# Casting transfers for v and z, paired half key tiles, and the experts' rows turned on VectorE

## The chip, the cores and the metric

The kernel runs on one core of a Trainium2 chip. TensorE multiplies, VectorE and ScalarE work on elements, GpSimd and SyncE (SP) issue transfers; GpSimd's queue also carries the gathers and scatters of the experts' rows. The metric is the device time of one execution in microseconds (us). Before the change three executions took 2464.53, 2465.4 and 2467.0 us: a median of 2465.4.

## What is computed

Eight batches of 2496 rows go through an attention without softmax, and then all 19,968 rows through a mixture of eight experts, each of which takes exactly 2496 rows.

```python
scores = (1.0 / S) * np.matmul(z, z.transpose(0, 2, 1))     # z: 8 x 2496 x 64
attn   = np.maximum(scores, 0.0) ** 2
x      = (u * np.matmul(attn, v)).reshape(B * S, D)         # u, v: 8 x 2496 x 256
logits = x @ w_gate                                         # 256 x 8
# the (row, expert) pairs in falling order of logit; a row goes to the first
# expert that still has room (room for N // E = 2496 rows each)
for e in range(E):
    mask = assigned == e
    h = np.maximum(x[mask] @ w1[e], 0.0)                    # 256 x 1024
    out[mask] = h @ w2[e]                                   # 1024 x 256
```

Everything is fp32.

## The kernel before

**Precision.** An fp32 operand is split into a high part, rounded to float32r, and a low part, the difference. A product is three matmuls: high by high, high by low, low by high. In the names `vh`, `vl`, `hi`, `lo`, `xh`, `xl` the h and l stand for the parts.

**Attention.** A batch has 20 key tiles: 19 of 128 rows and a last one of 64 (`NT` = 19, `TL` = 64). Queries go in five groups, four of 512 columns and one of 448. For each of the 40 groups and 20 key tiles there is a step n. `scores` multiplies key tiles in pairs, since the contraction has only 64 rows: one tile on rows 0 to 63 of the array, one on rows 64 to 127 (L961), three matmuls each. `rectify` takes the scores from PSUM, on ScalarE (L973) or VectorE (L971); ScalarE squares (L977); `split_hi` and `split_lo` make `hi` (L982 on ScalarE, L984 on VectorE) and `lo` (L993). `av` multiplies with v into two accumulators `acc`, one for each half of v's 256 columns (L1006, L1008, L1009). Of the half key tile the scores stand twice, on rows 0 to 63 and on 64 to 127; `split_lo` turns rows 64 to 127 of `hi` into the low part in place (L990), and `av` takes vh by both at once and vl by hi: four matmuls over 128 rows.

All scores of a group are issued in one burst of 60 matmuls, `LA` = 4 steps ahead of its first `av`. `hi` and `lo` have `LA` + 1 = 5 buffers. v and z of the next batch are split while the last query group of a batch runs: `load_v` and `load_z` fetch on SP, `split_v` rounds `vh` on ScalarE (L943) and subtracts `vl` on VectorE (L944), `split_z` likewise (L935, L936). `vh` and `vl` have `RING` = 22 buffers for 20 tiles. In that group the `hi` of even tiles is made on VectorE. After a group, VectorE turns the result in 32x32 blocks (`turn_acc`, L1015), multiplies with u (L1021), and SP writes it to `xd` in DRAM and reads it back as rows `xs`, of which VectorE makes eight logits per tile (`post_logits`, L1045). In the attention the order on TensorE, ScalarE and VectorE is the order in which this code is written (`manual_schedule`); the lists `todo` and `first_in` say at which step the loads, splits and logits stand. The order on SP and GpSimd is a scheduler's.

**Experts.** Each expert has 5 groups of rows with 8 steps each: 320 steps in all. GpSimd gathers a group's rows from `xd` (`gather_x`, L590, 4 gathers of 128 rows), TensorE transposes them into PSUM (`turn_x`, L642, 8 transposes into `xp` and `hp`), ScalarE and VectorE split them (L646, L647). A step computes a tile of the hidden layer in `hp` (L652 to L654), splits it (L730, L732) and, three steps later, multiplies it into `y` (L745 to L750). `put_y` adds the parts of y on VectorE (L773) and GpSimd scatters the rows (L781). Beside that VectorE and TensorE work out which rows the next expert gets (`route`: L124, L286 to L289, L523, L529 and others). The number of that expert comes into `which`, and `load_w` fetches its weights on SP. `todo` gives the step of each gather, turning and split; the scheduler sets the order within, and some operations are tied behind the last `hl` (L732) by `issue_after(paced[-1].ins)`.

## Time and profile before

| | |
|---|---|
| median of three executions | 2465.4 us (2464.53 to 2467.0) |
| profiled execution | 2466.28 us, span 2464.5 us |
| mean granted TensorE clock | 0.996 |
| TensorE busy | 2416.7 us, 98% |
| VectorE busy | 2067.0 us, 84% |
| ScalarE busy | 1535.1 us, 62% |
| GpSimd busy | 362.5 us, 15% |

The page gives busy times over the whole span, the chain of work that ended last (each instruction is followed back to what released it), and the costliest groups of instructions. Busy is not the same as limiting: an engine may be 84% busy over the span, and full in one stretch and half idle in another. The trace answers by stretch: busy time of each engine in a window, the single instructions with their starts, and who waited for whom. A wait counts only if it lies on the engine that sets the end.

### The profile page before, as it was taken

How to read it: one execution, taken by the hardware profiler on the slowest of the kernel's cores; microseconds unless marked ns; L12 is line 12 of the kernel's file. 1: busy time of each engine (PE TensorE's matmuls, PEld its weight loads, DVE VectorE, ACT ScalarE, POOL GpSimd, SP SyncE). 2: the span in 40 equal slices, each digit the busy share in tenths (PEclk: the TensorE clock that was granted, in tenths of full speed). 3: DMA queues.
4: the chain of work that ended last, by engine and by line, in shares of the span. 5: the costliest groups of instructions: out<-in, count | busy, mean ns of one | idle time of the engine just before them, and what ended most of it. 6: DMA issues, size and time to landing. Idle time of an engine off the chain costs nothing.

```text
span 2464.5 us, 42329 instructions
## 1 busy us (share of the span) xinstructions
PE 2416.7 (98%) x14948; PEld 2016.6 (82%) x14948; DVE 2067.0 (84%) x6309; ACT 1535.1 (62%) x2986; POOL 362.5 (15%) x508
## 2 busy tenths in 40 slices
PE   8999999999999999999999899999999999999997
PEld 6888888888888888888887787788888888888886
DVE  7899898998999998989989897879796969696332
ACT  7898888898898988888987123333333333343332
POOL 3000000000000000000000022233242433333332
PEclk9999999999999999999999999999999999999999
DMA  4132131131131321312211022121212111122111
GB/s 150 34 105 62 52 114 30 53 110 52 45 109 37 100 66 52 114 27 55 76 52 43 9 70 69 34 73 47 70 51 69 44 64 54 45 86 68 43 42 34
DMA packets 156852, 154.86 MB, mean 63 GB/s; under 512 B 89440, under 2 KB 129888, under 8 KB 156512
## 3 DMA queue, kind: packets, MB, share of 16 engines
q1 hardware_dynamic: 141408, 110.72, 15.1%
q0 software_dynamic: 15232, 41.44, 5.3%
q8 instruction: 117, 1.92, 0.3%
q14 instruction: 95, 0.78, 0.1%
HBM read 111.22 MB, written 40.89 MB: 62 GB/s over the span
## 4 chain that ended last, share of the span: by engine, by line
PE 86%; DVE 8%; issue 3%; ACT 1%; DMA 1%; POOL 1%; POOLq 0%; ACTq 0%; DVEq 0%; SPq 0%
PE acc L1006 14%; PE acc L1009 14%; PE acc L1008 13%; PE sc L961 10%; PE y L748 10%; PE hp L652 5%; PE hp L653 5%; PE y L750 5%; PE hp L654 5%; PE srch L281 1%; DVE lo L993 1%; PE srch L529 1%; DVE vl L944 1%; DVE mask L124 1%; DVE lt L1045 1%
## 5 line engine op out<-in xcount | busy, mean ns | idle before, releaser
L1006 PE MATMUL acc<-hi,vh 128*128 128x512 f32 (+1 forms) x1600 | 621.0, 388 | 2.8 <-DVE hi L984 2.7
L1009 PE MATMUL acc<-hi,vl 128*128 128x512 f32 (+1 forms) x1600 | 615.9, 385 | 0.0
L1008 PE MATMUL acc<-lo,vh 128*128 128x512 f32 (+1 forms) x1520 | 586.8, 386 | 0.2 <-DVE lo L993 0.2
L993 DVE TENSOR_TENSOR lo<-r,hi 128x512 fp32r<-128x512 f32 (+1 forms) x760 | 510.5, 674 | 55.9 <-ACT hi L982 50.2
L730 ACT ACTIVATE hh<-hp 128x512 fp32r<-128x512 f32 (+1 forms) x319 | 187.2, 587 | 592.1 <-PE hp L654 474.1
L982 ACT ACTIVATE hi<-r 128x512 fp32r<-128x512 f32 (+1 forms) x701 | 454.3, 648 | 112.6 <-ACT r L977 65.0
L977 ACT ACTIVATE r<-r 128x512 f32<-128x512 f32 (+1 forms) x800 | 505.5, 643 | 2.7 <-DVE r L971 2.5
L1045 DVE SCALAR_TENSOR_TENSOR lt<-xs,wgb 128x256 bf16<-128x256 f32 x1248 | 473.4, 419 | 1.9
L748 PE MATMUL y<-w,hh 128*128 128x512 f32 x1216 | 447.7, 400 | 2.2 <-DVE y L773 1.4
L1006 PEld LDWEIGHTS acc<-hi,vh 128*128 128x128 f32 x1600 | 300.8, 188 | 72.9 <-issue 14.5
L973 ACT ACTIVATE r<-sc 128x512 f32<-128x512 f32 (+1 forms) x638 | 314.0, 614 | 53.5 <-PE sc L961 52.5
L1009 PEld LDWEIGHTS acc<-hi,vl 128*128 128x128 f32 x1600 | 300.8, 188 | 55.1 <-DVE vl L944 0.2
L1008 PEld LDWEIGHTS acc<-lo,vh 128*128 128x128 f32 x1520 | 285.8, 188 | 56.0 <-DVE lo L993 5.0
L748 PEld LDWEIGHTS y<-w,hh 128*128 128x128 f32 x1216 | 228.3, 188 | 51.7 <-DVE y L773 2.6
L652 PE MATMUL hp<-xh,w1h 128*128 128x512 f32 (+2 forms) x642 | 256.7, 400 | 2.1 <-DVE hl__30375 L732 1.3
L590 POOL DMA_INDIRECT xg<-xd,idx x160 | 176.7, 1104 | 540.4 <-issue 244.7
L961 PE MATMUL sc<-z,z 64*128 64x512 f32 (+1 forms) x1920 | 243.6, 393 | 8.9 <-DVE r L971 5.8
L653 PE MATMUL hp<-xl,w1h 128*128 128x512 f32 (+2 forms) x642 | 251.1, 391 | 0.1
L654 PE MATMUL hp<-xh,w1l 128*128 128x512 f32 (+2 forms) x642 | 249.0, 388 | 0.0
L961 PEld LDWEIGHTS sc<-z,z 64*128 64x128 f32 x1920 | 197.3, 185 | 48.5 <-issue 11.7
L256 POOL IOTA slot<- 128x256 bf16 x1 | 1.5, 1531 | 1346.4 <-DVE nrem L366 1346.4
L781 POOL DMA_INDIRECT out_dram<-y,idx x160 | 163.5, 1022 | 195.8 <-DVE y L773 111.6
(1180 smaller groups left out, 3173.6 us busy)
## 6 DMA issues: line engine op xcount, KB each, us to landing
ur<-in_u_dram SPq DMA_DIRECT2D x39, 512.0 KB, 3.9
vr<-in_v_dram SPq DMA_DIRECT2D x32, 512.0 KB, 3.9
xd<-tr SPq DMA_DIRECT2D x128, 128.0 KB, 2.3
xs<-xd SPq DMA_DIRECT2D x32, 512.0 KB, 4.5
wr<-in_moe_w_dram SPq DMA_DIRECT2D x32, 512.0 KB, 4.9
zr<-in_z_dram SPq DMA_DIRECT2D x40, 256.0 KB, 3.0
xd<-tr SPq DMA_DIRECT2D x28, 112.0 KB, 2.1
vr<-in_v_dram SPq DMA_DIRECT2D x8, 384.0 KB, 3.4
```

The costliest lines, as they stand in the source:

```text
L652: nc.tensor.matmul(p[:, c], wh, xh, start=(d == 0), stop=False)
L653: nc.tensor.matmul(p[:, c], wh, xl, start=False, stop=False)
L654: latest["mm"] = nc.tensor.matmul(p[:, c], wl, xh, start=False, stop=(d == DH - 1))
L748: nc.tensor.matmul(o, h[:, c], w.rearrange("p s d -> p (s d)"), start=(f == 0), stop=(f == FT - 1), skip_group_check=True)
L961: nc.tensor.matmul(pair[s], key[b, p][r, c * 128:c * 128 + 128], query[b, g][r, :w], start=key is ZH and query is ZH, stop=key is ZL)
L977: nc.scalar.activation(R[n], R[n], AF.Square)
L982: nc.scalar.activation(h, R[n], AF.Copy)
L993: recent["l"] = nc.vector.tensor_sub(l, a, h.bitcast(F32))
L1006: nc.tensor.matmul(o, vh, h, start=(kt == 0), stop=False)
L1008: nc.tensor.matmul(o, vh, l, start=False, stop=False)
L1009: nc.tensor.matmul(o, vl, h, start=False, stop=last)
L1045: nc.vector.scalar_tensor_tensor(t[r], XS[b, g][r, i], 1.0, WG["rows"][r, e], op0=OP.mult, op1=OP.mult, accum_out=lg[r, j, e:e + 1])
```

## The change

1. From the second batch on, the high parts of v and z are no longer rounded by ScalarE. GpSimd issues transfers that cast on their way from DRAM: one for each full v tile, two for the half one, one for each of the five z tiles of a batch. The plain transfers of v and z stay, since the low parts are subtracted from them, four steps later than before (`low_v`, `low_z`); these plain loads are issued later.
2. The half key tile gets a `lo` tile of its own, and six matmuls of 64 rows in three pairs: the first half of v's columns on rows 0 to 63, the second on rows 64 to 127.
3. All `hi` of the last query group are made by ScalarE.
4. The 64 rows left over from an even and an odd batch are joined in one tile `tail` and give their logits together (24 products fewer for the six joined batches); the steps of the logits are shared out anew.
5. In 38 of the 40 expert groups the transposes in TensorE go. VectorE turns the gathered rows in 32x32 blocks (`tip_x`, L652 of the changed kernel), SP stores them in four transfers to a DRAM tile `flat` such that the blocks come to their places, reads them back (L658) as `xt`, and `split_x` splits from there (L665, L666). The turning stands 8 steps ahead of the group (7 for one group), the split 4; before, turning and split stood 6 ahead. `xg`, `tr` and `xt` have one buffer each.

The core of the diff:

```diff
@@ -621,7 +621,7 @@
                     nc.vector.tensor_sub(l, src, h.bitcast(F32))
 
         def gather_x(k, g):
-            t = fp.tile([128, 4, D], F32, name="xg")
+            t = fp.tile([128, 4, D], F32, name="xg", bufs=1)
             idx = ROUTE[k]["idx"]
             if g > (1 if k == 0 else 0):
                 with tc.issue_after(paced[-1].ins):
...
@@ -645,6 +645,26 @@
                 XL[k, g, d] = fp.tile([128, 512], F32R, name=f"xl{d}")[:, :w]
                 nc.scalar.activation(XH[k, g, d], t[d][:, :w], AF.Copy)
                 nc.vector.tensor_sub(XL[k, g, d], t[d][:, :w], XH[k, g, d].bitcast(F32))
+
+        def tip_x(k, g):
+            tr = fp.tile([128, 2 * 4, 4, 32], F32, name="tr", bufs=1)
+            with tc.issue_after(paced[-1].ins):
+                nc.vector.transpose(tr.rearrange("p b t j -> p t b j"), XG[k, g].rearrange("p t d -> p (t d)"))
+            flat = dram.tile([D, 512], F32, name="flat", bufs=2)
+            for a in range(4):
+                nc.sync.dma_start(flat[:, 128 * a:128 * a + 128].rearrange("(b i) n -> i b n", i=32),
+                                  tr[32 * a:32 * a + 32].rearrange("i b t j -> i b (t j)"))
+            XT[k, g] = fp.tile([128, DH, 512], F32, name="xt", bufs=1)
+            nc.sync.dma_start(XT[k, g], flat.rearrange("(h p) n -> p h n", h=DH))
+
+        def split_x(k, g):
+            for d in range(DH):
+                src = XT[k, g][:, d].rearrange("p (a t j) -> p t a j", a=4, t=4)
+                hl = [fp.tile([128, 512], F32R, name=f"{n}{d}") for n in ("xh", "xl")]
+                h, l = [t.rearrange("p (t a j) -> p t a j", t=4, a=4) for t in hl]
+                nc.scalar.activation(h, src, AF.Copy)
+                nc.vector.tensor_sub(l, src, h.bitcast(F32))
+                XH[k, g, d], XL[k, g, d] = [t[:, :width(g)] for t in hl]
 
         def expand_part(k, g, f, p, c, d):
             wh, wl = [t[:, d, f % 4] for t in W1[k, f // 4]]
...
@@ -797,7 +817,11 @@
                 n0 = (k * NG + g) * FT
                 if n0:
                     at(1 if (k, g) == (0, 1) else n0 - AHEAD + (LATE if (k, g) == (1, 0) else 0), gather_x, k, g)
-                    at(n0 - 4 if (k, g) == (0, 1) else n0 - 6, turn_x, k, g, range(DH))
+                    if (k, g) == (0, 1):
+                        at(n0 - 4, turn_x, k, g, range(DH))
+                    else:
+                        at(n0 - (7 if (k, g) == (1, 0) else 8), tip_x, k, g)
+                        at(n0 - 4, split_x, k, g)
                 at(n0 + FT - 1, put_y, k, g)
             n0 = k * PER
             for h in range(2):
...
@@ -931,18 +955,29 @@
         def split_z(b, g):
             ZZ[b, g] = zp.tile([128, 2, 512], F32R, name=f"z{g}", bufs=1 if g else 2)
             ZH[b, g], ZL[b, g] = ZZ[b, g][:, 0], ZZ[b, g][:, 1]
-            src = ZI.pop((b, g))
-            return (nc.scalar.activation(ZH[b, g], src, AF.Copy),
-                    nc.vector.tensor_sub(ZL[b, g], src, ZH[b, g].bitcast(F32)))
+            if b:
+                nc.gpsimd.dma_start(ZH[b, g], z[b, :, 512 * g:512 * g + 512])
+                return
+            return nc.scalar.activation(ZH[b, g], ZI[b, g], AF.Copy), low_z(b, g)
+
+        def low_z(b, g):
+            return nc.vector.tensor_sub(ZL[b, g], ZI.pop((b, g)), ZH[b, g].bitcast(F32))
 
         def split_v(b, kt):
-            src = VR[b, kt // 4][:, kt % 4]
-            h = vp.tile([128, D], F32R, name="vh")
-            l = vp.tile([128, D], F32R, name="vl")
-            with in_turn(b):
-                nc.scalar.activation(h, src, AF.Copy)
-                nc.vector.tensor_sub(l, src, h.bitcast(F32))
-            VH[b, kt], VL[b, kt] = h, l
+            VH[b, kt] = vp.tile([128, D], F32R, name="vh")
+            if b == 0:
+                with in_turn(b):
+                    nc.scalar.activation(VH[b, kt], VR[b, kt // 4][:, kt % 4], AF.Copy)
+                    low_v(b, kt)
+            elif kt < NT:
+                nc.gpsimd.dma_start(VH[b, kt], v[b, 128 * kt:128 * kt + 128])
+            else:
+                for c in range(2):
+                    nc.gpsimd.dma_start(VH[b, kt][c * TL:(c + 1) * TL], v[b, 128 * kt:])
+
+        def low_v(b, kt):
+            VL[b, kt] = vp.tile([128, D], F32R, name="vl")
+            nc.vector.tensor_sub(VL[b, kt], VR[b, kt // 4][:, kt % 4], VH[b, kt].bitcast(F32))
 
         seq = [(b, g, kt) for b in range(B) for g in range(NQ) for kt in range(KT)]
 
...
@@ -978,7 +1013,7 @@
 
         def split_hi(n):
             h = wk.tile([128, 512], F32R, name="hi", bufs=LA + 1)[:, :width(seq[n][1])]
-            if n >= KT and (seq[n][1] != NQ - 1 or n % 2 or n == B * NQ * KT - 2):
+            if n >= KT:
                 nc.scalar.activation(h, R[n], AF.Copy)
             else:
                 nc.vector.tensor_copy(h, R[n])
...
@@ -986,27 +1021,26 @@
 
         def split_lo(n):
             a, h = R.pop(n), HI[n]
-            if seq[n][2] == NT:
-                nc.vector.tensor_sub(h[TL:], a[TL:], h[TL:].bitcast(F32))
-                return
-            l = wk.tile([128, 512], F32R, name="lo", bufs=LA + 1)[:, :width(seq[n][1])]
-            recent["l"] = nc.vector.tensor_sub(l, a, h.bitcast(F32))
-            LO[n] = l
+            LO[n] = wk.tile([128, 512], F32R, name="lo", bufs=LA + 1)[:, :width(seq[n][1])]
+            recent["l"] = nc.vector.tensor_sub(LO[n], a, h.bitcast(F32))
 
         def av(n):
             b, g, kt = seq[n]
             if kt == 0:
                 ACC[b, g] = [ps.tile([128, 512], F32, name=f"acc{d}", bufs=1) for d in range(2)]
-            last = kt == NT
-            h, l = HI.pop(n), LO.pop(n, None)
-            for d in range(2):
-                o = ACC[b, g][d][:, :width(g)]
-                c = slice(d * 128, (d + 1) * 128)
-                vh, vl = VH[b, kt][:, c], VL[b, kt][:, c]
-                nc.tensor.matmul(o, vh, h, start=(kt == 0), stop=False)
-                if not last:
-                    nc.tensor.matmul(o, vh, l, start=False, stop=False)
-                nc.tensor.matmul(o, vl, h, start=False, stop=last)
+            o = [ACC[b, g][d][:, :width(g)] for d in range(2)]
+            c = [slice(d * 128, (d + 1) * 128) for d in range(2)]
+            h, l, vh, vl = HI.pop(n), LO.pop(n), VH[b, kt], VL[b, kt]
+            parts = ((vh, h), (vh, l), (vl, h))
+            if kt < NT:
+                for d in range(2):
+                    for i, (w, x) in enumerate(parts):
+                        nc.tensor.matmul(o[d], w[:, c[d]], x, start=(kt == 0 and i == 0), stop=False)
+                return
+            for i, (w, x) in enumerate(parts):
+                for d in range(2):
+                    r = slice(d * TL, (d + 1) * TL)
+                    nc.tensor.matmul(o[d], w[r, c[d]], x[r], start=False, stop=(i == 2))
 
         def turn_acc(b, g):
             w = width(g)
...
@@ -1031,18 +1065,18 @@
             n = w // 128
             nc.sync.dma_start(XS[b, g][:, :n], xd[lo:lo + 128 * n].rearrange("(i p) d -> p i d", p=128))
             if n < 4:
+                if b % 2 == 0:
+                    TAIL[b // 2] = wk.tile([128, D], F32, name="tail", bufs=1)
                 r = TL * (b % 2)
-                nc.sync.dma_start(XS[b, g][r:r + TL, n], xd[lo + 128 * n:lo + w])
+                nc.sync.dma_start(TAIL[b // 2][r:r + TL], xd[lo + 128 * n:lo + w])
 
         def post_logits(b, g, i, e):
             if 4 * g + i < NT:
-                r = slice(0, 128)
-                j = b * NT + 4 * g + i
+                r, src, j = slice(0, 128), XS[b, g][:, i], b * NT + 4 * g + i
             else:
-                r = slice(TL, 128) if b % 2 else slice(0, TL)
-                j = B * NT + b // 2
+                r, src, j = slice(0, 128 if b % 2 else TL), TAIL[b // 2], B * NT + b // 2
             t = wk.tile([128, D], BF, name="lt")
-            nc.vector.scalar_tensor_tensor(t[r], XS[b, g][r, i], 1.0, WG["rows"][r, e], op0=OP.mult, op1=OP.mult,
+            nc.vector.scalar_tensor_tensor(t[r], src[r], 1.0, WG["rows"][r, e], op0=OP.mult, op1=OP.mult,
                                            accum_out=lg[r, j, e:e + 1])
 
         def last_cut(i):
...
@@ -1153,11 +1190,13 @@
             if b:
                 for g in range(NQ):
                     m = n0 - KT + (0, 4, 8, 12)[g - 1] if g else n0 - KT - 8
-                    at(m - 8, load_z, b, g)
+                    at(m - 2, load_z, b, g)
                     at(m + 1, split_z, b, g)
-                    at(n0 - KT + 4 * g - 8, load_v, b, g)
+                    at(m + 5, low_z, b, g)
+                    at(n0 - KT + 4 * g - 4, load_v, b, g)
                 for kt in range(KT):
                     at(n0 - KT + kt, split_v, b, kt)
+                    at(n0 - KT + kt + 4, low_v, b, kt)
             else:
                 for kt in range(KT):
                     at(kt - 4, split_v, 0, kt)
```

**GpSimd's queue from the first batch on.** Before, its constants are followed at once by the experts' work (L590 gathers, L781 scatters):

```order
L242 IOTA idi 64x4
L243 IOTA idi 64x4
L780 MEMSET spacer 1x1 x160
L256 IOTA slot 128x256
L294 CAST hq<-ones_j 128x512
L590 DMA xg<-xd,idx 128x256 x12
L781 DMA out_dram<-y,idx 19968x256 x4
```

In the changed kernel the casting transfers of a batch stand there (L959 for z, L973 for full tiles of v, L976 for the half one):

```order
L973 DMA vh<-in_v_dram 128x256 x2
L959 DMA z_3985<-in_z_dram 128x512
L959 DMA z_2049<-in_z_dram 128x512
L959 DMA z_2110<-in_z_dram 128x512
L959 DMA z_2177<-in_z_dram 128x512
L959 DMA z_2246<-in_z_dram 128x512
L973 DMA vh<-in_v_dram 128x256 x17
L976 DMA vh<-in_v_dram 64x256 x2
L973 DMA vh<-in_v_dram 128x256 x2
```

The last row holds the first two tiles of the batch after; then that batch's z follows.

**TensorE at the end of a query group.** Before, the half key tile is four matmuls, behind a full tile's six (of which the last is shown) and ahead of the next scores (L961):

```order
L1009 MATMUL acc_223<-hi,vl 128x512
L1006 MATMUL acc_222<-hi,vh 128x512
L1009 MATMUL acc_222<-hi,vl 128x512
L1006 MATMUL acc_223<-hi,vh 128x512
L1009 MATMUL acc_223<-hi,vl 128x512
L961 MATMUL sc<-z_170 128x512 x12
```

In the changed kernel the full tile's matmuls have the line L1038, and those of the half tile L1043:

```order
L1038 MATMUL acc_223<-hi,vl 128x512
L1043 MATMUL acc_222<-hi,vh 128x512
L1043 MATMUL acc_223<-hi,vh 128x512
L1043 MATMUL acc_222<-lo,vh 128x512
L1043 MATMUL acc_223<-lo,vh 128x512
L1043 MATMUL acc_222<-hi,vl 128x512
L1043 MATMUL acc_223<-hi,vl 128x512
```

The two accumulators now take turns, so that neighbours lie on different rows of the array.

**VectorE in an expert.** Before, around the split of a group's rows (`xl`, L647) stand the low parts of the hidden layer (`hl`, L732) and the search for the next expert's rows (L286 to L289, L410 and on):

```order
L732 SCALAR_TENSOR_TENSOR hl__24937<-hp,hh 128x512
L286 TENSOR_TENSOR hd<-srch,diag 128x7x16
L288 TENSOR_REDUCE hr<-hd 128x7
L289 TENSOR_TENSOR hx<-hr,dE 128x8x7
L732 SCALAR_TENSOR_TENSOR hl__24975<-hp,hh 128x512
L647 TENSOR_TENSOR xl_24997<-xp,xh_24996 128x512
L647 TENSOR_TENSOR xl_25001<-hp,xh_25000 128x512
L410 SCALAR_TENSOR_TENSOR best<-srch,step_17865 128x8x7
```

In the changed kernel the turning of that group's rows (L652), between an `hl` (now L752) and a step of the search:

```order
L286 TENSOR_TENSOR hd<-srch,diag 128x7x16
L288 TENSOR_REDUCE hr<-hd 128x7
L289 TENSOR_TENSOR hx<-hr,dE 128x8x7
L752 SCALAR_TENSOR_TENSOR hl__24972<-hp,hh 128x512
L652 STREAM_TRANSPOSE tr<-xg 128x4x8x32
L410 SCALAR_TENSOR_TENSOR best<-srch,step_17948 128x8x7
```

And the split of the same group, four `hl` further on:

```order
L752 SCALAR_TENSOR_TENSOR hl__25119<-hp,hh 128x512
L628 MEMSET xg 1x4
L410 SCALAR_TENSOR_TENSOR best<-srch,step_17948 128x8x3
L415 TENSOR_REDUCE Dg<-best 128x1
L379 TENSOR_TENSOR T<-W,Dg 128x3
L394 TENSOR_TENSOR V<-V,Dg 128x1
L666 TENSOR_TENSOR xl_25131<-xt,xh_25130 128x512
L666 TENSOR_TENSOR xl_25135<-xt,xh_25134 128x512
```

VectorE's queue has one instruction more per group, and the split stands later than before, closer to the matmuls that need it.

## Rows read from the trace of the kernel before

**Rows 1.** The page: TensorE's busy time, and the chain by engine.

```profile
PE 2416.7 (98%) x14948; PEld 2016.6 (82%) x14948; DVE 2067.0 (84%) x6309; ACT 1535.1 (62%) x2986; POOL 362.5 (15%) x508
PE 86%; DVE 8%; issue 3%; ACT 1%; DMA 1%; POOL 1%; POOLq 0%; ACTq 0%; DVEq 0%; SPq 0%
```

**Rows 2.** Windows: stretch, length; busy PE, PEld, DVE, ACT, POOL; clock; DMA share, GB/s.

```profile
286.93:321.16 34.23, 34.23 (x180) 27.98 (x180) 31.29 (x104) 28.90 (x55) 0.00 (x0) 1.00 0.19 55
321.16:355.24 34.08, 34.08 (x202) 29.98 (x203) 32.93 (x88) 32.74 (x76) 0.00 (x0) 1.00 0.44 139
355.24:388.10 32.86, 32.10 (x160) 25.67 (x156) 30.15 (x105) 28.33 (x53) 0.00 (x0) 1.00 0.22 61
```

**Rows 3.** TensorE's waits, 1700 to 2220: us in total, times, longest.

```profile
PE srch L281 <- DVE mask L124: 0.4, 1, 0.4
```

**Rows 4.** Windows in an expert.

```profile
1872.00:1885.00 13.00, 13.00 (x86) 10.88 (x85) 7.97 (x23) 3.48 (x6) 1.35 (x2) 1.00 0.06 21
1911.00:1963.00 52.00, 51.91 (x422) 44.73 (x420) 51.24 (x128) 18.19 (x34) 20.41 (x17) 1.00 0.13 42
```

**Rows 5.** The chain, 284 to 324: start, us, what.

```profile
286.02 0.23 PE acc L1006
...
286.93 7.26 PE sc L961 x59
```

**Rows 6.** The chain, 330 to 336, in a 448-wide group.

```profile
329.81 0.20 PE acc L1009
...
335.69 0.21 PE acc L1008
```

**Rows 7.** TensorE's waits, 52 to 1339.

```profile
PE sc L961 <- DVE r L971: 5.8, 8, 0.8
```

**Rows 8.** VectorE's lines, 321.16 to 355.24: count, busy us, mean ns, idle.

```profile
L944 DVE TENSOR_TENSOR vl<-vr,vh 128x256 fp32r<-128x256 f32 x19 | 8.0, 419 | 0.0
...
L984 DVE CAST hi<-r 128x448 fp32r<-128x448 f32 x8 | 3.1, 387 | 0.0
```

**Rows 9.** ScalarE's lines, 321.16 to 355.24.

```profile
L943 ACT ACTIVATE vh<-vr 128x256 fp32r<-128x256 f32 x20 | 9.0, 450 | 0.0
...
L982 ACT ACTIVATE hi<-r 128x448 fp32r<-128x448 f32 x8 | 4.9, 614 | 0.0
```

**Rows 10.** TensorE's timeline, 1351 to 1356: start, us, what, [idle before, releaser].

```profile
1352.26 0.47 PE L1006 MATMUL acc<-hi,vh 128*128 128x448 f32 x1 [2.68 <-DVE hi L984]
```

**Rows 11.** GpSimd's timeline, 1730 to 1740 and 1786 to 1792.

```profile
1733.74 0.96 POOL L590 DMA_INDIRECT xg<-xd,idx  x1 [0.30 <-issue]
1735.01 0.95 POOL L590 DMA_INDIRECT xg<-xd,idx  x1 [0.30 <-issue]
...
1786.90 1.56 POOL L590 DMA_INDIRECT xg<-xd,idx  x1 [0.30 <-issue]
1788.76 1.50 POOL L590 DMA_INDIRECT xg<-xd,idx  x1 [0.30 <-issue]
```

**Rows 12.** The page's transfers: count, KB each, median us to landing.

```profile
xd<-tr SPq DMA_DIRECT2D x128, 128.0 KB, 2.3
xs<-xd SPq DMA_DIRECT2D x32, 512.0 KB, 4.5
```

**Rows 13.** VectorE's timeline, 1785 to 1792.

```profile
1786.07 1.55 DVE L523 TENSOR_TENSOR ob<-rab,slot 128x1280 bf16<-128x1280 bf16 x2
```

**Rows 14.** The chain, 1974 to 1984, in an expert.

```profile
1978.89 0.44 PE xp L642 x4
```

**Rows 15.** VectorE's lines, 321.16 to 355.24: the turning of results.

```profile
L1015 DVE STREAM_TRANSPOSE tr<-acc 128x512 f32<-128x512 f32 x2 | 1.3, 692 | 0.0
...
L1015 DVE STREAM_TRANSPOSE tr<-acc 128x448 f32<-128x448 f32 x1 | 0.6, 639 | 0.0
```

**Rows 16.** The chain, 1780 to 2060: one step of the search, an expert apart.

```profile
1788.19 1.02 PE srch L529 x40
...
1915.32 1.02 PE srch L529 x40
```

More of the change, by code (lines that the diff above doesn't have):

```diff
@@ L66, in tile_attention_then_moe @@
     attention(tc, u, ut, v, z, w_gate, gate_rows, xd, identf, made, first, 1.0 / S)
-    moe(tc, xd, first, jp, identf, w1, w2, out, B, S, consts)
+    moe(tc, xd, first, jp, identf, w1, w2, out, B, S, consts, dram)
 def best_expert(nc, first, c, eq):
@@ L133, in spread, with moe @@
     nc.vector.tensor_copy(rep[:, h:], x[:, h:, None].to_broadcast([128, n - h, 8]))
-def moe(tc, xd, first, jp, identf, w1, w2, out, B, S, cp):
+def moe(tc, xd, first, jp, identf, w1, w2, out, B, S, cp, dram):
     nc = tc.nc
@@ L585, in moe @@
         w2v = w2.rearrange("e (c p q) d -> e p c q d", c=2, p=128)
-        W1, W2, WR, XG, XH, XL, HH, HL, HP, YP = {}, {}, {}, {}, {}, {}, {}, {}, {}, {}
+        W1, W2, WR, XG, XT, XH, XL, HH, HL, HP, YP = {}, {}, {}, {}, {}, {}, {}, {}, {}, {}, {}
         scat = []
@@ L893, in attention @@
         ZZ, ZH, ZL, ZI, VR, VH, VL, UR = {}, {}, {}, {}, {}, {}, {}, {}
-        XS, ACC, TR, SC, R, HI, LO, XT = {}, {}, {}, {}, {}, {}, {}, {}
+        XS, ACC, TR, TAIL, SC, R, HI, LO, XT = {}, {}, {}, {}, {}, {}, {}, {}, {}
         recent = {}
@@ L1118, in at, with logits_at @@
             todo.setdefault(n, []).append((f, a))
-        def logits_at(m0):
-            n = m0 // KT - 1
+        def logits_at(b, g):
+            n = b * NQ + g
+            m0 = (n + 1) * KT
             if n == B * NQ - 2:
                 return [m0 + 4 + i // 2 for i in range(4 * E)]
-            own, go, late = ((11, 12, 9), (16, 12, 4), (20, 10, 2), (0, 14, 18), (6, 14, 12))[n % NQ]
+            own, go, late = ((8, 14, 10), (14, 12, 6), (22, 10, 0), (0, 14, 18), (4, 14, 14))[g]
             if n == B * NQ - 3:
-                own, go, late = 20, 12, 0
+                own, go = 20, 12
+            if g == NQ - 1 and b % 2 == 0 and b + 2 < B:
+                own, go, late = 4, 12, 8
             return ([m0 + 8 + i * 12 // max(own, 1) for i in range(own)] + [m0 + KT] * go
@@ L1143, in attention @@
                     first_in[m0].insert(0, (times_u, (b, g)))
-                for e, n in enumerate(logits_at(m0) if m0 < B * NQ * KT else ()):
+                for e, n in enumerate(logits_at(b, g) if m0 < B * NQ * KT else ()):
                     first_in.setdefault(n, []).append((post_logits, (b, g, e // E, e % E)))
```

## The prediction, made before the changed kernel ran

> **What bounds the kernel now.** I read the page's busy shares and its chain first: TensorE is busy 98% of the span and carries 86% of the chain that ended last, VectorE 8% [rows 1]. A microsecond taken from TensorE is therefore worth a microsecond, as long as nobody falls behind it. So I went on to the busy times by stretch. In a 512-wide query group of the attention TensorE fills all 34.23 us; VectorE works 31.29 and ScalarE 28.90 of them. The batch's last group, 448 wide, is where the next batch's v and z are split, and there VectorE (32.93 of 34.08) and ScalarE (32.74) nearly fill it too. The group behind it is the one in which TensorE is not full, 32.10 of 32.86 [rows 2]. In the experts TensorE waits 0.4 us for others in 520 us [rows 3], while VectorE's load swings: 7.97 of 13 us in one stretch, 51.24 of 52 in another [rows 4].
>
> The profiled execution took 2466.28 us: its span of 2464.5 and 1.8 around it. It lies 0.9 above the median of 2465.4; I sum against it and take 0.9 off at the end.
>
> **The half key tile.** It costs four full-height matmuls, from 286.02 to 286.93: 0.91 us, 0.227 each [rows 5]. Now it takes six matmuls of 64 rows, in three pairs whose halves sit on different rows of the array. The trace has such pairs, the scores: 30 pairs (59 of 60 are recorded) in 7.26 us [rows 5], 0.242 a pair. Three pairs are 0.73, and 0.18 goes. In the eight 448-wide groups a matmul takes 0.203 (329.81 to 335.69 are 29 of them [rows 6]), and about 0.16 goes. 32 x 0.18 + 8 x 0.16 = 7 us. Bounds: 8.9 gone, if a pair costs one matmul (0.227 x 40 less a little for the narrow ones); 18 more than before, if pairs did not overlap (six by 0.227 are 1.36, so +0.45 x 40). I take 7, since the scores show it.
>
> **The batch boundary.** At the start of a batch's second group TensorE waits for VectorE's scaled scores, eight times, 5.8 us in all and 0.8 at most [rows 7]. VectorE comes late out of the group before, behind its casts (8 in the stretch shown, at 387 ns) and the low parts of v (19 at 419 ns) [rows 8]. All ten casts of that group go to ScalarE: 10 x 0.37 = 3.7 us less on VectorE, and four low parts move on into the next group. 3.7 covers 0.8 with room. What could be late next there is ScalarE, but it gives up 20 copies of vh at 450 ns, 9.0 us, and the z copies, and gets 10 hi copies at 614, 6.1 [rows 9]; it ends lighter too. I take 5 of 5.8; bounds 0 and 5.8. VectorE also has 24 fewer products for the logits; TensorE was full beside them, so nothing.
>
> **The end of the attention.** TensorE stands 2.68 us at 1352.26 behind VectorE's cast, and its next matmul takes 0.47 [rows 10] where 0.203 is the rule. With the casts gone VectorE arrives some 3 us earlier, but the products queued ahead of the low part stay. I take 2 us; bounds 0 and 4 (the wait, and half of it again in slow matmuls).
>
> **The casting transfers.** They decide the sign. GpSimd does nothing in the attention before; now it issues, in every batch's last group, 5 transfers for z, 17 and two halves for v, then two that belong to the batch after (the order is shown with the change). No direct transfer by GpSimd is in the trace. The nearest rows are its gathers of 128 rows of 1 KB: in a burst the starts 1733.74 and 1735.01 lie 1.27 apart; elsewhere 1786.90 and 1788.76 lie 1.86 apart [rows 11]. What they meet: TensorE frees one v buffer per key tile, every 6 x 0.203 = 1.22 us, 18 of them in 21.9; the z buffers come free when the last scores are done, four tiles (4 x 6 x 0.227 = 5.4 us) ahead of the group. So 24 transfers of a slot s meet 27.3 us. The cover has three parts. A low part of v stands four steps behind its transfer, and VectorE cannot reach it sooner than five tiles after the buffer came free, since hi has five buffers: 6.1 us, less one issue (1.3) and a landing of 2.3 [rows 12], leaves 2.5. TensorE has up to four finished tiles in hand: 4.9. And between this group's tiles 15 and 16 it runs the next group's scores, 7.3 us, in which GpSimd catches up. 24s - 27.3 - 14.7 is negative up to s = 1.75. At 1.27 all is hidden; at 1.86 a batch loses 2.6 us and seven lose 18. I take 1.27, the slot for the same volume and the same 1 KB rows, and keep 1.86, and above it the last rival below.
>
> Here a page speaks. The Trainium skill, "SBUF — State Buffer", section "Who interferes with whom", says that a VectorE copy or cast in a two-port mode keeps GpSimd from writing its descriptors, and that an operation with two SBUF inputs hinders only a GpSimd instruction which reads SBUF. The trace agrees as far as it goes: VectorE's neighbour of the slow gathers is a product of two SBUF operands [rows 13], and a gather reads its index list. By that page a direct transfer, with no list, in a group rid of its casts goes at the undisturbed slot, and the sum stays at 1.27. By the rows alone 1.86 is as possible, since VectorE's lo and vl have two SBUF inputs all through that group.
>
> **The experts' rows.** Eight transposes in TensorE go in 38 of 40 groups. Four take 0.44 us in the chain, and a like piece of four follows [rows 14]: 0.88 x 38 = 33.4 us, all on the path. Instead VectorE turns 128x1024 in blocks. The nearest rows are 692 ns for 512 columns and 639 for 448 [rows 15]: 53 ns for 64, so 692 + 8 x 53 = 1.12 us, or twice 692 = 1.38; I take 1.2. Then come four stores of 128 KB and a read of 512 KB on SP's queue, 2.3 and 4.5 us to landing [rows 12], with the issues some 9 us in all. Between the turning and the split lie four steps. An expert has 40 steps in 127.1 us [rows 16], without its transposes 122.7, so four are 12.2. The split's copy and subtraction are as long as before. The path is hidden by 3 us. Once per expert the read stands on SP behind the load of the expert's number and a weight transfer; the number is made about a dozen VectorE instructions behind the turning, so I count nothing, with 3 us an expert (21 in all) as its bound.
>
> VectorE must find 5 x 1.2 = 6 us an expert. From 1911 to 1963 it is busy 51.24 of 52 us [rows 4]: with two groups' transposes gone the same work must end 1.75 us sooner, and holds 2.4 more. 51.2 + 2.4 - 50.25 = 3.4 us too much. TensorE runs about one step (3.1) ahead of what it needs from VectorE; I count 2.8 of it as cushion, so 0.6 an expert shows: seven experts, 4 us. Bounds 0 and 7 x 3.4 = 24.
>
> **Sum.** -7 - 5 - 2 + 0 - 33.4 + 4 = -43.4: 2422.9 against the profiled execution, 2422 against the median.
>
> **Rivals.**
> *VectorE takes the gain in the experts (0.22).* The cushion is already spent where VectorE is full [rows 4], or the read waits behind the weights. For it: 51.24 of 52. Against: 0.4 us of waits in 520 [rows 3], so with VectorE that full there was still slack. Price 20 us more than the forecast: 2442. Half tiles that do not overlap, 7 + 18 = 25 more or 2447, are counted here.
> *Slots near 1.9 us (0.10).* As worked out: 2440 at 1.86, and level with before where a batch loses 43/7 = 6.2 us, at s = (42 + 6.2)/24 = 2.0.
> *The casting transfers hold the queue until they land (0.18).* Issued one by one, each when the last had landed, their slot would be the landing's 2.3 us [rows 12]. A batch would lose 24 x 2.3 - 42 = 13 us in its last group: VectorE stands at a low part of v, the next lo parts and scaled scores queue behind it, and TensorE waits for those. Seven batches are 92 us: 2514, slower. It decides from 2.0 us a slot. For it: no casting transfer is in the trace. Against: the gathers start 1.27 apart, less than a landing, so several are under way at once. The Trainium skill ("DMA: Bandwidth & Descriptors", section "Anatomy of one DMA — SWDGE (gpsimd) path") puts the fixed part of a GpSimd transfer at some 2.0 us, mostly the receipt of the written data; were that its slot, the estimate by that page would be level with before. No run here shows it.
>
> **How the numbers follow.** The forecast has 0.50, its own range 2413 (no price in the experts, the far bounds of the attention's three terms) to 2433 (half of the bound in the experts). What a measurement can't tell from no change is 0.2%, 4.9 us. Faster: 0.50 + 0.22 + 0.04 of the slots near 1.9, 0.76. Same: 0.05, where the slot comes out at 2.0. Slower: the rest, 0.19. The range goes from 2408 to 2470: some 0.03 lies below it, 0.16 above.
>
> **What would show it.** In a last group GpSimd's transfers start about 1.3 us apart, and VectorE has no idle time ahead of the low part of v; were the last rival true, it waits there for a DMA, TensorE behind it for lo and scaled scores, and the group grows beyond 40 us. The half tile: 0.73 us from its first matmul to the next operation. The batch boundary: no wait of 0.8 us for scaled scores. In the experts: a period of 122.7 us plus what TensorE waits for hl, xl or xh; the turning at 1.1 to 1.4 us; the read landed before the split is reached. The forecast is wrong if the last group grows at all, or if an expert's period stays above 125.

## The result

The changed kernel takes 2432.5 us (2431.3 to 2434.3, four runs), before 2465.1 beside it: a ratio of 0.9866, 95% interval 0.9851 to 0.9881, so 33 us faster. The forecast was 2422, in a range of 2408 to 2470. The profiled execution took 2432.56 us, 2430.5 of them span.

### The profile after

The page, as in [rows 1]: TensorE has 37 us less to do and is still busy 98% of the span, but its share of the chain that ended last fell from 86 to 82%, and VectorE's rose from 8 to 10.

```profile
PE 2380.0 (98%) x14724; PEld 1983.2 (82%) x14724; DVE 2068.5 (85%) x6220; ACT 1521.4 (63%) x2890; POOL 460.6 (19%) x690
PE 82%; DVE 10%; issue 4%; POOL 1%; ACT 1%; DMA 1%; POOLq 0%; DVEq 0%; SPq 0%; ACTq 0%
```

The attention is best compared from one burst of scores to the next. First before, three stretches: a 512-wide group, the 448-wide one, and the one behind the batch boundary (start and end, length, busy PE, PEld, DVE, ACT, POOL, then the granted clock and what the transfers did, as in [rows 2]).

```profile
252.61:286.86 34.25, 34.25 (x180) 28.45 (x180) 32.32 (x113) 30.13 (x56) 0.00 (x0) 1.00 0.17 47
321.09:352.46 31.37, 31.37 (x180) 27.62 (x180) 30.22 (x82) 30.39 (x71) 0.00 (x0) 1.00 0.43 135
352.46:388.02 35.56, 34.80 (x180) 28.02 (x180) 32.85 (x111) 30.67 (x58) 0.00 (x0) 1.00 0.25 71
```

The same three groups after:

```profile
251.20:285.24 34.04, 34.04 (x184) 28.22 (x182) 32.48 (x117) 30.13 (x56) 0.00 (x0) 1.00 0.17 47
319.09:349.85 30.76, 30.76 (x184) 27.76 (x182) 27.49 (x68) 27.82 (x56) 12.70 (x24) 1.00 0.88 230
349.85:384.49 34.64, 34.64 (x184) 27.59 (x182) 31.51 (x107) 30.25 (x57) 0.54 (x1) 1.00 0.37 101
```

An ordinary group lost 0.21 us, the 448-wide one 0.61, and the one behind the boundary 0.92. TensorE is no longer short there (34.64 of 34.64, before 34.80 of 35.56). VectorE and ScalarE, which had 30.2 and 30.4 of 31.4 us in the 448-wide group, have 27.5 and 27.8 of 30.8.

GpSimd in that group, its timeline (start, duration, what, the idle time before and its releaser): the casting transfers cost 0.53 us each, and from the second v tile on the queue waits 0.69 us before each one for TensorE to free a buffer.

```profile
327.36 0.53 POOL L973 DMA_DIRECT2D vh<-in_v_dram  x1 [2.08 <-PE acc L1038]
328.57 0.53 POOL L973 DMA_DIRECT2D vh<-in_v_dram  x1 [0.69 <-PE acc L1038]
329.79 0.53 POOL L973 DMA_DIRECT2D vh<-in_v_dram  x1 [0.69 <-PE acc L1038]
```

TensorE's waits from 52 to 1339, as in [rows 7] and [rows 10] (us in total, times, longest): of the eight waits for scaled scores, the seven at a batch boundary (0.73 to 0.77 us each) are gone, and the one left, 0.6 us, stands in the first batch. But the 2.7 us in the last group of all are still there, now behind `lo`.

```profile
PE acc L1038 <- DVE lo L1025: 2.7, 1, 2.7
PE sc L996 <- DVE r L1006: 0.6, 1, 0.6
```

In the experts the same step of the search, as in [rows 16], lies 125.64 us apart, not 127.13 (the four such distances from 1639.80 on are 127.4, 125.6, 125.7 and 127.0), and the stretch before the boundary between two experts (as the second of [rows 4]) has TensorE at 50.49 of 52 us while VectorE has 51.39:

```profile
1767.21 1.02 PE srch L529 x40
...
1892.85 1.03 PE srch L529 x40
```

```profile
1880.00:1932.00 52.00, 50.49 (x390) 42.66 (x389) 51.39 (x124) 20.27 (x36) 17.85 (x16) 1.00 0.39 125
```

From 1700 to 2140 TensorE's waits are these; [rows 3] had 0.4 us in a longer stretch:

```profile
PE srch L281 <- DVE mask L124: 5.7, 3, 1.9
PE y L768 <- DVE y L793: 0.5, 3, 0.2
```

And VectorE's turning is the size that was estimated, 1.23 us:

```profile
L652 DVE STREAM_TRANSPOSE tr<-xg 128x1024 f32<-128x1024 f32 x5 | 6.2, 1234 | 0.0
```

### The profile page after: what moved, and what is told of

Its sections match the earlier page's. It is cut to its first block, busy times and chain, and to the rows that moved or that the text cites. A ratio compares the mean times of both kernels' runs of the same rounds, so it can differ in the third digit from the quotient of the medians.

```text
span 2430.5 us, 42677 instructions
## 1 busy us (share of the span) xinstructions
PE 2380.0 (98%) x14724; PEld 1983.2 (82%) x14724; DVE 2068.5 (85%) x6220; ACT 1521.4 (63%) x2890; POOL 460.6 (19%) x690
## 4 chain that ended last, share of the span: by engine, by line
PE 82%; DVE 10%; issue 4%; POOL 1%; ACT 1%; DMA 1%; POOLq 0%; DVEq 0%; SPq 0%; ACTq 0%
PE acc L1038 41%; PE sc L996 11%; PE y L768 8%; PE hp L672 4%; PE hp L674 4%; PE hp L673 4%; PE y L770 4%; PE srch L281 2%; PE acc L1043 1%; POOL xg L590 1%; DVE mask L124 1%; DVE ob L523 1%; DVE w1l L621 1%; PE xp L325 1%; PE srch L529 1%
## 5 line engine op out<-in xcount | busy, mean ns | idle before, releaser
L1025 DVE TENSOR_TENSOR lo<-r,hi 128x512 fp32r<-128x512 f32 (+1 forms) x800 | 536.1, 673 | 83.1 <-ACT hi L1017 80.1
L1038 PE MATMUL acc<-hi,vh 128*128 128x512 f32 (+1 forms) x1520 | 590.8, 389 | 0.2 <-ACT vh L970 0.2
L1038 PE MATMUL acc<-lo,vh 128*128 128x512 f32 (+1 forms) x1520 | 587.7, 387 | 2.7 <-DVE lo L1025 2.7
L1038 PE MATMUL acc<-hi,vl 128*128 128x512 f32 (+1 forms) x1520 | 585.9, 385 | 0.0
L1017 ACT ACTIVATE hi<-r 128x512 fp32r<-128x512 f32 (+1 forms) x780 | 500.2, 641 | 122.1 <-ACT r L1012 87.0
L1079 DVE SCALAR_TENSOR_TENSOR lt<-xs,wgb 128x256 bf16<-128x256 f32 x1192 | 449.2, 417 | 0.0
L1038 PEld LDWEIGHTS acc<-hi,vh 128*128 128x128 f32 x1520 | 286.2, 188 | 67.0 <-issue 13.8
L1038 PEld LDWEIGHTS acc<-lo,vh 128*128 128x128 f32 x1520 | 286.3, 188 | 59.2 <-DVE lo L1025 8.2
L1038 PEld LDWEIGHTS acc<-hi,vl 128*128 128x128 f32 x1520 | 286.3, 188 | 52.1
L590 POOL DMA_INDIRECT xg<-xd,idx x160 | 181.2, 1133 | 513.3 <-DVE xg L628 281.1
L996 PE MATMUL sc<-z,z 64*128 64x512 f32 (+1 forms) x1920 | 236.9, 389 | 4.2 <-ACT z L961 2.8
L959 POOL DMA_DIRECT2D z<-in_z_dram x35 | 18.7, 534 | 960.0 <-DVE lt L1079 530.0
```

The source lines that it names most:

```text
L590: return nc.gpsimd.indirect_dma_start(out=dst, out_offset=None, in_=src, in_offset=bass.IndirectOffsetOnAxis(ap=idx, axis=0))
L996: nc.tensor.matmul(pair[s], key[b, p][r, c * 128:c * 128 + 128], query[b, g][r, :w], start=key is ZH and query is ZH, stop=key is ZL)
L1017: nc.scalar.activation(h, R[n], AF.Copy)
L1025: recent["l"] = nc.vector.tensor_sub(LO[n], a, h.bitcast(F32))
L1038: nc.tensor.matmul(o[d], w[:, c[d]], x, start=(kt == 0 and i == 0), stop=False)
L1079: nc.vector.scalar_tensor_tensor(t[r], src[r], 1.0, WG["rows"][r, e], op0=OP.mult, op1=OP.mult, accum_out=lg[r, j, e:e + 1])
```

## The experiments

All ratios are to the kernel before, run beside each. The changed kernel stood at 0.9866 (0.9850 to 0.9883) in the second series as well. The series ran with before at 2461.0, 2467.0 and 2467.7 us, so I compare ratios and give the difference to the changed kernel from them.

**The two halves apart (e1).** The new `attention` beside the old `moe`; the diff is the one shown, without the functions inside `moe`.

> The changed attention with the experts of before. If the two halves of the change are independent, the time is before less what the trace of after has gained when the experts' part begins (the last attention group's scores start 16.2 us sooner, the first routing matmuls L564 16.8 us sooner): 2465.1 - 16.8 = 2448. If the new expert part gains more than the traces say and the attention less (for instance through the transfers that reach into the experts' start), it comes out above 2452.

Measured: 2439.1 us, 0.991 (0.9894 to 0.9927), 21.9 us below before. So the new attention is worth about 22 us to the whole kernel where 14 were forecast, and of the 33 us of transposes only some 11 arrive (0.991 - 0.9866; 5 to 16 by the intervals). One expert of this kernel, and the same one of the changed kernel:

```profile
1767.25:1894.22 126.97, 126.87 (x898) 106.78 (x896) 104.40 (x301) 42.55 (x80) 43.97 (x41) 1.00 0.18 58
```

```profile
1767.21:1892.85 125.64, 123.39 (x859) 102.58 (x856) 109.32 (x306) 42.49 (x81) 43.54 (x41) 1.00 0.33 101
```

TensorE has 3.5 us less to do; the expert gets 1.3 shorter, and TensorE stands still for 2.25 of it. VectorE has 4.9 us more.

Where the 11 us arrive, the two traces show. From the first routing step (L564) to the last step of the search (L529), and from there to the end, first e1, then the changed kernel:

```profile
1402.20:2231.70 829.50, 821.74 (x6036) 690.01 (x6036) 696.17 (x1958) 275.65 (x515) 279.14 (x256) 1.00 0.19 60
2231.70:2437.25 205.55, 196.08 (x1054) 168.17 (x1052) 73.76 (x151) 62.52 (x124) 61.95 (x65) 0.99 0.13 42
```

```profile
1403.87:2231.59 827.72, 804.22 (x5797) 667.24 (x5796) 727.93 (x1989) 275.40 (x515) 277.30 (x256) 0.99 0.32 98
2231.59:2430.46 198.87, 189.40 (x990) 160.88 (x988) 81.25 (x158) 62.28 (x124) 64.39 (x65) 0.98 0.29 85
```

Behind the search VectorE works 81 of 199 us; TensorE has 6.7 us less to do there, and the stretch is 6.7 shorter. While the search runs TensorE has 17.5 us less to do, and the stretch is only 1.8 shorter: TensorE stands still for 23.5 us of it, in e1 for 7.8.

**Is it VectorE, or the way through DRAM? (e2 to e4).** Three edits that should tell: the turning copied on ScalarE, `xl` subtracted on GpSimd, and one group in five left to TensorE.

```diff
-nc.vector.transpose(tr..., XG[k, g]...)
+nc.scalar.activation(tr..., XG[k, g]..., AF.Copy)      # e2
-nc.vector.tensor_sub(l, src, h.bitcast(F32))
+nc.gpsimd.tensor_sub(l, src, h.bitcast(F32))           # e3, in split_x
-if (k, g) == (0, 1): at(n0 - 4, turn_x, ...)
+if g == 1: at(n0 - 4 if k == 0 else n0 - 6, turn_x, ...)   # e4
```

> The changed kernel, where ScalarE copies the gathered rows to tr instead of VectorE turning them: the rows are not transposed, all transfers, waits and matmuls stay. Theory V (VectorE is full for some 50 us of each expert, and its five turnings of 1.23 us make TensorE wait there): VectorE has 6.2 us less per expert, the gaps of 2 to 3 us per expert close, and most of the 16 us given back returns: about 2418. Rival D (the path of gather, store to DRAM and reading back makes the split late): nothing changes on that path, 2432 within 3.

Measured: 2519.0 us, 1.0239 (1.0222 to 1.0256). A flaw of the experiment, not an answer: ScalarE's queue is in order, and the copy waits there for the gather (33 times, 182 us in all) while the hidden layer's `hh` queue behind it. From ScalarE's timeline:

```profile
1902.19 1.06 ACT L652 ACTIVATE tr<-xg 128x1024 f32<-128x1024 f32 x1 [6.20 <-DMA xg<-xd,idx]
1903.15 1.07 ACT L750 ACTIVATE hh<-hp 128x512 fp32r<-128x512 f32 x2
```

> The changed kernel with the low parts xl of the experts' rows subtracted on GpSimd (now possible, since the rows lie in SBUF). Theory V: VectorE loses ten operations of 0.68 us per expert, so 2418 to 2424, as long as GpSimd makes one in under 3 us beside its gathers. Rival D: no gain; with GpSimd's queue longer by ten operations the gathers come later and it is slower, 2435 or more.

Measured: 2555.0 us, 1.0381 (1.0364 to 1.0399). GpSimd takes 1.34 us for what VectorE does in 0.68, mostly behind its gathers, and TensorE waits for it 48 times. Like e2 it says nothing on the theory. GpSimd's line, and TensorE's wait:

```profile
L666 POOL TENSOR_TENSOR xl<-xt,xh 128x512 fp32r<-128x512 f32 x74 | 97.4, 1340 | 73.6 <-ACT xh L665 72.8
```

```profile
PE hp L673 <- POOL xl L666: 81.7, 48, 4.4
```

> The changed kernel, but the second group of rows of every expert is turned by TensorE as before: 7 experts more with eight transposes (0.88 us), and one turning of 1.23 us less on VectorE, in the stretch where it is full. Theory V: TensorE pays 7 x 0.88 = 6 us and its waits shrink by up to 7 x 2.1 = 15: 2424 to 2430. Rival D, if that group's round trip is not the late one: plus 6, 2438; if it is the late one, 2424 too, but then e2 shows no gain.

Measured: 2438.6 us, 0.9904 (0.9887 to 0.992), some 9 us above the changed kernel. I had taken the wrong group. The turnings in the full stretch start at 1899.46 and 1927.50; they are those of an expert's fifth group and of the next one's first. The second group's falls where VectorE has room, so TensorE paid and got nothing back, and lost 5.8 us waiting for gathers as well.

**The load on VectorE alone (e5 to e7).** The changed kernel again (e5); each turning cut to a quarter (e6); each made twice (e7).

```diff
-nc.vector.transpose(tr (all), XG[k, g] (all))
+nc.vector.transpose(tr[:, :, 0], XG[k, g][:, 0])       # e6; ScalarE writes
+nc.scalar.activation(tr[:, :, 1:], identf..., AF.Copy) # a constant elsewhere
+nc.vector.transpose(tr (all), XG[k, g] (all))          # e7: a second time
```

> The changed kernel itself, as the reference of the other runs on this chip. By its ratio to before (0.9866) some 33 us below before.

> The changed kernel with VectorE turning only a quarter of each group's rows (128x256); ScalarE writes a constant over the rest of tr. The rows are not all transposed; stores, read and split stay. VectorE has about 5 x 0.8 = 4 us less per expert, some 1.7 to 2.5 of it in the full stretch. Theory V (VectorE full there sets the pace): 1.7 to 2.5 us an expert come back, 12 to 18 us below the changed kernel. Rival D (the way through DRAM, or where the new operations stand in the order, makes TensorE wait): within 3 us of the changed kernel.

> The changed kernel with each turning on VectorE made twice (1.23 us more for each of 38 groups, 6.2 us an expert, 2 to 3 of the five in the full stretch). Theory V: 2.5 to 3.7 us an expert slower, 17 to 26 us above the changed kernel. Rival D: the read comes 1.2 us later where the way has 3 us to spare; within 4 us of it.

Measured: 2434.0, 2422.4 and 2464.8 us; 0.9866, 0.9818 (0.9802 to 0.9834) and 0.9988 (0.9979 to 0.9998). With 0.8 us less for each turning, 11.6 us come back; with 1.24 more, 31 are lost, almost the whole gain. Neither edit touches TensorE's matmuls, and the stores, the read and the split are the same in all three. TensorE's wait for the search's masks, from 1700 to 2140 (e7: 2170), in e6 and then in e7:

```profile
PE srch L281 <- DVE mask L124: 2.9, 6, 1.1
```

```profile
PE srch L281 <- DVE mask L124: 15.1, 3, 5.0
```

VectorE's load sets the pace here, and the way through DRAM has room in the changed kernel: only in e7, where the stores stand 1.24 us later, does TensorE wait for the split's `xh`, 0.55 us an expert. The expert shown above for e1 and the changed kernel, in e6 and then in e7:

```profile
1762.66:1887.65 124.99, 123.36 (x854) 102.49 (x853) 104.90 (x306) 45.95 (x85) 44.58 (x40) 1.00 0.34 101
1775.01:1906.39 131.38, 125.12 (x854) 103.72 (x853) 114.24 (x311) 42.44 (x82) 43.90 (x41) 0.99 0.31 96
```

The mean of four such periods is 127.2 us in e5, 124.8 in e6 and 131.8 in e7: 6.2 us more for VectorE in an expert cost 4.6, and 4 us less give 2.4 back.

Not all of this is waiting. The same 14,724 matmuls keep TensorE busy for 2372.7 us in e6, 2378.2 in e5 and 2389.1 in e7, with a mean granted clock of 0.997, 0.994 and 0.988. Once per expert of e7 TensorE stands still for some 5 us, and behind it the granted clock is 0.50, the lower of its two levels (1.2 GHz, not 2.4), for 3.4 or 6.8 us; e6 has no such stretch between 1540 and 2413. So a part of what VectorE's load costs arrives as slower matmuls. One of these waits of e7, and the stretch in which the clock is low (third figure from the end):

```profile
1950.70 0.53 PE L281 MATMUL srch<-mask,oh 128*128 128x112 bf16 x4 [5.00 <-DVE mask L124]
```

```profile
1948.83:1955.65 6.82, 4.95 (x23) 4.55 (x23) 6.82 (x21) 0.73 (x2) 0.00 (x0) 0.50 0.45 125
```

**Another pace for the search (e8).**

```diff
-want = -(-(pos - starts[k] + 1) * YIELDS // (end - starts[k]))
+x = (pos - starts[k] + 1) / (end - starts[k])
+# y: straight lines through (0, 0), (0.25, 0.16), (0.7, 0.73), (1, 1)
+want = -(-y * YIELDS // 1)          # for k > 1
```

> The changed kernel with the search for the next expert's rows paced otherwise, from the third expert on: slower in the first quarter of an expert's steps (0.16 of the work instead of 0.25), faster up to 0.7 of them (0.73), so that VectorE's work in its full stretch is spread into the slack one. Theory V: the gaps of 2 to 3 us shrink in five experts, 5 to 12 us below the changed kernel. Rival D: no change, or slower where the search's matmuls then wait.

Measured: 2454.4 us, 0.9946 (0.9929 to 0.9962), 20 us above the changed kernel. The masks' wait did shrink (in e5 it is 10.8 us, 3.3 at the longest), but a new one came, once per expert: TensorE waits for the split's `xh`, 2.5 us at the longest, and behind it the clock is 0.50 for 6.8 us in each of four experts. TensorE's waits from 1400 on, and SP's timeline at one of them:

```profile
PE hp L672 <- ACT xh L665: 11.4, 5, 2.5
PE srch L281 <- DVE mask L124: 7.3, 8, 1.3
```

```profile
1882.65 0.80 SPq L655 DMA_DIRECT2D flat<-tr  x2
1885.78 2.32 SPq L599 DMA_DIRECT2D wr<-in_moe_w_dram  x4
1888.15 0.96 SPq L655 DMA_DIRECT2D flat<-tr  x2
1894.84 0.38 SPq L658 DMA_DIRECT2D xt<-flat  x1
```

Two of the four stores (L655) stand behind the next expert's weights, and the read is issued 13.5 us behind the turning at 1881.39; in the changed kernel it is 6.0 (1875.58 to 1881.54). The prediction had priced the read behind these weights at up to 3 us an expert. Why the stores came behind the weights, no run shows: `which` is made 2.9 us behind the turning here, and 3.6 in the changed kernel.

**The right group on TensorE (e9).** The first group of each expert, whose turning lies in the full stretch.

```diff
-if (k, g) == (0, 1):
+if (k, g) == (0, 1) or g == 0:
     at(n0 - 4, turn_x, k, g, range(DH))
```

> The changed kernel, but the first group of every expert is turned by TensorE (four steps ahead): of the two turnings on VectorE that fall into its full stretch one goes. An expert takes 125.7 us now. Theory V: VectorE's bound falls by 1.23 to 124.5, TensorE's work rises by 0.88 to 123.6; so 1.2 us for each of seven experts, 8 us below the changed kernel: a ratio to before of 0.983. Rival: the cost is in TensorE's waits for particular matmuls whose place in the order moves with every edit; then anywhere between 6 below and 10 above it.

Measured: 2422.7 us, 0.9823 (0.9807 to 0.984), some 11 us below the changed kernel, past the 6 that the rival allowed: 56 transposes more on TensorE, and the fastest version here that computes the whole result, ahead of both kernels. The masks' wait from 1700 to 2140 is 1.5 us, and the clock is full from 1543 to 2412:

```profile
PE srch L281 <- DVE mask L124: 1.5, 4, 0.5
```

**The attention's parts (e10 to e12).** The half tile as before; the casts back on VectorE; each transfer of v cut into four of 64 columns.

```diff
 # e10: split_lo and av as in the kernel before
-if n >= KT:
+if n >= KT and (seq[n][1] != NQ - 1 or n % 2 or n == B * NQ * KT - 2):   # e11
-nc.gpsimd.dma_start(VH[b, kt], v[b, rows])
+for c in range(4):                                                       # e12
+    nc.gpsimd.dma_start(VH[b, kt][:, q(c)], v[b, rows, q(c)])
```

> The changed kernel with the half key tile as before (four matmuls over 128 rows). If the pairs are worth 0.20 us a group, as the two traces' group periods say (34.25 and 34.05), 40 x 0.20 = 8 us above the changed kernel, a ratio to before of 0.990. If the periods differ for another reason (VectorE or the transfers), no change: 0.9866.

Measured: 2439.0 us, 0.9884 (0.9868 to 0.9901): 4 us above the changed kernel, less than the two intervals can tell apart. The profile tells it: the 512-wide group takes 34.25 us again, to the hundredth.

```profile
252.48:286.73 34.25, 34.25 (x179) 28.46 (x178) 32.60 (x117) 30.13 (x56) 0.00 (x0) 1.00 0.17 47
```

> The changed kernel with the hi of even tiles of the last query group cast on VectorE again. Theory: these casts made VectorE late at the batch boundary; with vl's last four and some logits moved away VectorE has 27.5 of 30.8 us in that group now, and 10 x 0.37 = 3.7 more just fill it: 0 to 8 us above the changed kernel. By the Trainium skill (SBUF page, Who interferes with whom) the casts would also hold up GpSimd's casting transfers, whose 0.53 us would grow beside them; if they do not, the rule does not bite here.

Measured: 2437.7 us, 0.9878 (0.9861 to 0.9894): 3 us above, not told apart by the intervals. The 448-wide group takes 31.19 us in place of 30.76, and no wait at the boundary comes back, which was what I had blamed on the casts. GpSimd's transfers of v take 0.533 us in the mean, without the casts 0.530, and the 21 of v and z that started while such a cast ran took 0.53 too: the Trainium skill's rule on casts and descriptors ("SBUF — State Buffer", section "Who interferes with whom") does not show here in GpSimd's time. Whether the data land later, no run shows.

```profile
319.45:350.64 31.19, 31.19 (x184) 27.80 (x182) 30.35 (x78) 23.74 (x49) 12.60 (x24) 1.00 0.86 227
```

> The changed kernel with each casting transfer of a full v tile split into four of 64 columns: the same bytes, 83 transfers on GpSimd per last group instead of 26. With a slot of 0.53 (its busy time) to 0.83 us (with the 0.30 that the gathers show between them) they take 44 to 69 us against 27.3 and a cover of 8 to 15: late by 2 to 33 us in each of seven batches, so 14 to 230 us above the changed kernel, and the wait shows on VectorE ahead of vl. Rival: several transfers are under way and the queue keeps up; no change, which would mean that the prediction's last rival was never near.

Measured: 2516.8 us, 1.0203 (1.0186 to 1.022), some 83 us above the changed kernel, 12 a batch. The chain of waits that the last rival described is real: once GpSimd is late, VectorE waits at `vl`, and TensorE for scaled scores and `lo`. What the rival rested on is not: the queue does not hold a transfer until it has landed, back to back they take 0.53 us each (13 in 6.87), and in the chain one lands 5.7 us behind its issue (at 349.85). TensorE stands still some 60 us longer in this attention than in the changed kernel's, and behind ten of its waits there the clock is 0.50 for 3.4 or 6.8 us. GpSimd's timeline, VectorE's waits and TensorE's waits:

```profile
338.71 6.87 POOL L975 DMA_DIRECT2D vh<-in_v_dram  x13 [0.19 <-issue]
```

```profile
DVE vl L982 <- DMA vh<-in_v_dram: 80.9, 49, 5.3
```

```profile
PE sc L998 <- DVE r L1008: 37.2, 8, 6.9
PE acc L1040 <- DVE lo L1027: 12.9, 11, 2.9
```

## Why the prediction came out as it did

The direction and the range held. The sum was 10 us too fast, and that it came so close is in part luck: the attention gave 8 us more than forecast, the experts' rows some 18 less.

**The half tile: right.** Forecast 7 us; 0.21 a group, 40 groups, are 8, and e10 brings the group's time back. The chain shows it badly: it gives the new tile 0.90 us, where [rows 5] gave the old one 0.91. Entering the 64-row pairs costs some 0.1 us once: the second pair starts 0.34 us behind the first, the third 0.23 behind the second.

```profile
284.38 0.50 PE L1043 MATMUL acc<-hi,vh 64*128 64x512 f32 x2
284.72 0.40 PE L1043 MATMUL acc<-lo,vh 64*128 64x512 f32 x2
284.95 0.40 PE L1043 MATMUL acc<-hi,vl 64*128 64x512 f32 x2
```

That step used to stand between the half tile and the first scores, which are pairs too, and now stands ahead of the half tile. One must compare whole periods.

**The batch boundary: right in place, too small, for the wrong reason.** I took the recorded waits, 5.8 us, for the whole loss. The two stretches around it lost 0.61 + 0.92 = 1.53 us a batch; without 0.2 each for the half tile 1.1 remains, about 8 us over the seven boundaries between batches. The 448-wide group lost its share though TensorE counts as busy through all of it before as well. And e11 gives the casts only 0.43 us a batch, all of it in that group; the wait behind the boundary went with something else that left the stretch (four `vl`, ScalarE's copies, the logits), which no run took apart.

**The end of the attention: wrong.** Forecast 2; the wait is 2.7 us as before, now for `lo`. VectorE's products in front of it, which I had named, and the masks ahead of them hold it without any cast. The matmul of 0.47 us was no sign of a slow one: matmul records last 0.36 to 0.47 us and start 0.203 apart, and I compared the two. What the wait does bring is the lower clock, for 3.4 us behind it in the trace of before and 6.8 in the changed kernel's. From the last group's first scores to the first routing step (L564) only 0.6 us went.

**The casting transfers: right, with a slot that was too long.** 1.27 us was taken from the gathers; a direct transfer holds GpSimd for 0.53. The cover was never tested in the changed kernel. It is in e12: 83 transfers by 0.53 to 0.60 are 44 to 50 us, which the formula would have charged with 2 to 8 us a batch; 12 were lost, some 9 of them as standstill of TensorE. The formula counted on the next group's scores between tiles 15 and 16; the trace has them behind the half tile [rows 5]. Without that part of the cover it gives 9 to 15.

**The experts' rows: the step that failed.** The transposes went, 33.4 us by [rows 14]. I charged 4 us for VectorE's load, since TensorE was to have a cushion of 2.8 us an expert; no row showed that cushion, and the bound of 24 was the better number. By e1 some 22 us of 33 are given back: VectorE was full for 52 us of each expert [rows 4], and TensorE waited so little there [rows 3] because the two happened to end together, not because there was slack. e6 and e7 show it from both sides: 6.2 us more on VectorE cost an expert 4.6, 4 us less give 2.4 back, and in e9 one turning moved out of the full stretch gives more than its transposes cost. TensorE waits for the search's masks, not for the `hl`, `xl` or `xh` that I had said to watch. A term was missing altogether: behind a wait the clock can fall, and the matmuls that follow take longer. The sign that I had set, an expert's period above 125 us, came true. The first rival named all this but the clock, with 20 us; its time of 2442 was missed because the attention gave more than forecast.

**What stays open.** The start of the experts, up to the second expert's list, is 4 us shorter in e1 than before, and the last expert 6 us, with the same code; the trace of before has 2.1 us of idle TensorE at 2286 to 2312 that e1 lacks. Before itself ran at 2461.0 us beside e1 and at 2465.1 beside the changed kernel, so a part of the 10 us may be no more than that difference. No run settles it, and with it how e1's 22 us divide; how much of the loss in the experts is the clock's, no run takes apart either.

## What to carry to other kernels

A stretch in which two engines are full has no slack just because neither waits for the other: count the load that a change adds to the second one, in that stretch, as paid. Then move work between them stretch by stretch: turning on VectorE pays where it has room, and on TensorE where it has none (e9). A wait in a list is a lower bound of a loss, since the clock can fall behind it; compare periods from the same event to the same event.

## What was not expected of the hardware

A casting transfer of 128x256 from DRAM holds GpSimd for 0.53 us, one of 128x64 for 0.53 to 0.60, and a gather of the same 128 rows for 0.95 to 1.56 [rows 11]. So cutting a transfer into four costs GpSimd about four times as much.

The clock does not fall behind every wait. The changed kernel has two waits of 1.90 us for the same mask in two experts, ending at 1932.57 and 2058.25: behind the first the clock stays full, behind the second it is 0.50 for 3.4 us, and 448-wide matmuls start 0.37 us apart instead of 0.20.
